# A new issue order for an attention, experts and mixing kernel whose instructions stay the same

## The chip, the cores and the metric

The kernel runs on one core of one Trainium2 chip. The metric is the device time of one execution in microseconds; where several executions are given, their median counts. The core has four compute engines that each work through their own stream of instructions in order: TensorE (PE, with its weight loads as PEld), VectorE (DVE), ScalarE (ACT) and GpSimd (POOL). SyncE (SP) issues transposing DMAs. They meet only at semaphores.

## The reference

Three layers follow one another, on 2 batches of 768 rows with 512 columns.

```python
# 1. attention of 8 heads (64 columns each) in which a query sees the keys of its own hash bucket
mask = q_bucket[:, :, :, None] == k_bucket[:, :, None, :]      # buckets: signs of q @ proj, k @ proj
scores = np.where(mask, scale * q @ k.T, -1e9); attn = softmax(scores); x = attn @ v
# 2. four causal attention experts (64 columns each), the best two of four weighted per row
logits = x @ w_gate;  y = sum over e of w_e * (softmax(causal(scale * (x@wq[e]) @ (x@wk[e]).T)) @ (x@wv[e])) @ wo[e]
# 3. channel mixing with the row before
xk = mu_k * y + (1 - mu_k) * y_prev; xr = mu_r * y + (1 - mu_r) * y_prev
out = sigmoid(xr @ w_r) * (np.maximum(xk @ w_k, 0) ** 2 @ w_v)
```

## The kernel before, in words

Numbers are split into a high and a low float16 part, and most products are three matmuls (high by high, high by low, low by high). Rows are worked on in 12 units of 128 (6 of each batch). A unit, with its number at the end of a tile's name, goes through these steps:

- `query_steps`: load q, split it (`naq`, `nbq`), turn it on PE (`tr_x2`, `tr_x1`) and copy it out by DVE (`x2`, `x1`). `key_steps` does the same for the keys of four heads (`nak`, `nbk`, `tr_y2`, `tr_y1`).
- `lsh_steps`: for each of 8 heads a score (`s`, 4 matmuls), the softmax (`softmax`: DVE reads the score out of PSUM into `P` with a running minimum, `mx`; ACT takes the exponential; ACT or POOL makes the high part of `PHL`, POOL the low part; an SP DMA transposes it into `PT`), then `pv` (`x`, 18 matmuls). `fin` divides and turns the result (`tr_x_`, `xT`).
- `moe_steps`: queries and keys of the experts (`proj_qk`: four groups of 12 matmuls, all in one tile `qk`, read out by ACT and DVE into `qT` and `kT`), values and gate (`vg`), scores (`se`), softmax, `pv` (`y`), `fin`, output (`o`).
- `mix_steps`: the shift (`m32k`, `m32r`, `mk`, `mr`), the hidden layer (`h`), the gate (`r`), the down product (`v`), the result `e`, and the store.
- `weight_steps`: weights are loaded and split once, by ACT, POOL and DVE (`split_w`, `split_d`).

PSUM has two pools. Scores (`s`, `se`) have two tiles of two banks each. Everything else that PE writes shares one tag with four tiles of one bank each:

```python
ps_s = Pool(... bufs=2, space=PSUM)   # [P, 2, 512] float32: two banks each
ps_d = Pool(... bufs=4, space=PSUM)   # [P, 512] float32: one bank each
```

In `turn`, a tile of up to 8 transposes is written in two halves of the same bank, and each half has its own copy:

```python
for j in range(2):
    for c in range(hn):
        nc.tensor.transpose(pt[j][:, c * P:(c + 1) * P], src[...], ident16)
    nc.vector.tensor_copy(dst[:, j * hn:(j + 1) * hn, :], pt[j]...)
```

In `fin` of `moe_steps` the sums of the softmax, their reciprocals (`rs`, profile name `y`) and the products with the gate (`rse`) use four columns of the bank of the tile `y`, into which `pv` accumulates.

Nothing of this is issued when it is written down. A `Program` records every instruction as an operation (consecutive matmuls of one step are one operation; there are 2673), and `arrange` reads a table, `ORDER`, which says in which order the operations are issued; `issue` then emits them at one line, so every row of the profile has line 188. An engine's stream is the table's operations of that engine, in the table's order. Dependences between engines become semaphore waits by that order. For a PSUM tile they go by bank: two accesses to the same bank by different engines are kept in the table's order, even where they touch different columns and neither needs the other's data. A wait stops all that stands behind it on its engine. All loads and stores are issued from ACT's stream (`LOADS = nc.scalar`), among its compute instructions.

Of the kernel before, what the change touches and what calls it, by code (L numbers as in the profile page):

```python
# [844 lines left out]
c-jru)3#tq5CG9cRc6&`+qP}r+qP}nwr$(CZQHhOyJvnOUiOOOPyhs?LKw&c`C%kX1OkA<&<65CJ}3wgp)HJp(J%(aLRy#vlVJ)JgXGW%3PBMl3gdtw1
VTXpAqsSZNYD|cLOX~I)1U;Dgmh2}N<#){4;{dOh4hdDQbJ?s4mH7nhg8r6hQfH50CiwGbb>N412RGYnV=kGhAa>bVnB3=30WZ<goT-q9l}F6hybzRHu
iv~&<uJ)4yXmapf>b{)KC}FKs<;Gi6IvZgM}~<VnaQM1M#6V+{2uZ1ae{mNR7Fn56ptzFdOdRU3`dTAr}sZE-(ic!3Y=xiy=4W!LHB`5<+uG1bHzZroq
857y3g*s02eG6K2NpkQUQnQb>;(uma4Xc`zUD<3`AWSuq<H#Rs?ql0kN?3XiZDR)dUK982I*D1Zg=F+RbkH~==mW+;T!p$3%1Wso03uqv*EYWM<Q;&OO
~^XWO}z{*es=F&W>i)FD4mclw%ms>z6u7JW=9k)OYTm`G4Cf34wxE1PS18j(m@D-NB()b$7<04uBKQIDqgDSXyDquydgb}GFMxw|Rg%(l~Tug7U39f-9
)DmjrPh3g|VJ-Z^sI(oF9IXRSZ}A<z$EFChjCR0sLRvx1F$Tq?m9&Z)V+;I^fABBX<N90~n_)m<h$tEzg8Hx%5>P8_jjdokBqXLbco^EEp|I2%jzBDmO  # L850
^GNDwZo&(kT-y(#PktAVRwv6$KU|<!p7W$cfmj04Sg^^HR5pe8B<bIJ`MwLHJyNtc#zgmGwy-S`6Tql6ttH5ViHP9d!Q%w!|QZ|4$&8Ek6-Z{?uCK4j@
FaV2Ks=Vuq$@MQ*atOU}x-t{c#_pp~IA%;?W=+jQe2(j>J(o8pq%`9FG%lBHpAS7@m^RWV{He=nM?Sv~+}y(pi{-Q*jzj$M1L!&cjaHMK|FRG~ji30fy
lLn2ED+HXf%FG#oF(6-Z6HDLSR2Ie3e%LJJ;?E%_GAz-y46GEhdk4GGL#Y{jj40p5Z0^bl^-Jj_KG=nhT7yKo)yQV8v#8*mR6VSY+%_R>iTrA@RLH&Z^
!N-v=yT%`N(2)58ZdH@CJ6fMEW@C5Et7J5LZsW26!r*MXjQ4U&&nJ6=5qgOB=3(;0uiqBvf7NLi<9A86rDoQ!&F7=bnyaKn;c6vr1;VgCGOH_s4z$1E0
Pv|w}rnivL6r()!4xYn)8o>?VJ-mQK<^#N>pRgKh(I@x}m+1;srB%2FSK?ai%H8-26sPrAjjB@(x<|j@H`J!*^pw8BMk+}gusnT(?@)q9@;2Owb*L_N=
O566U(r<xa3k)Z3RICs@o26@Z8(W3MWrd3*^U!9x!Hlca5w&eq~^XULw_L*Zo+>M76DV3lqQwgj9YLkzM*rJ+N3p)%tU@ci0Mpax<(D?EfLnFvNVY&^A
t{F+VVSkPvLM6?!$IGgBufLd+xvsI6O9_4^)nRQUr{MGdU90BZE!oftkg#+2S0Y%F}o+)+gru*pwQPU^8k??P(zYp@rOwe^Co+No}Y#wWW^SlVjsQQap
f$2eHFe<T0B$h)1v;4d%I=i5GEi9>a(5C?3P(2>h20V;}B7^LQ1PG{`IYHw|IS#63w^xfeMe%U#HGXNrtNISx+eVH|KL{!9<eV(w0TxgU3=PSk^zaCS4
C$MFgLLf`2VeWb56p5tOXjE_Gk0X{YTd4bJgzEOI!l%rr*ii(fT6I048=Y)6>FJVrT%j7oEIT0@7HGCPb;0lh0rA--A)|4{?_?dZb;&Kd*j$!zPS<Q(t
CdcB~JfGw6OA`ZQ;#$sN;&FUVzzI1Pp2n~oj>B^VZfMTnI*!P%Oh(hlWHOn}dVXUza3qe*Q8+4}#JA?Psc1HG5=@Gxu#!28=diKqO-Z<kX=--yLVF&Yn  # L860
Jgw5C*{R9)Lg);cnuSAG){)eF$ESjDe<ehjzvsSQ_LjhnkE(Az%9I+znSl*yt#>$O%+qs<T1s~R^H6DOma@adpRZV=d5OttzmZXPVPpVcpGo$Y9_C#ZG
M<KCZAbim)d3a0H@;oW*?{K<@OraHHW#LDPRhkLZ*T_$cOlkIl_DRD5v2Sc9p%uce#XVVeavL&cHv-FO!~E+O*u#jHYz_*Bs;He1hAWlibdn=6~iCH#c
p}7`o2YO)Ha;Gjlf1%USshU*y$xjRlLAY>3Iuaco?>)~>Vf%vnCi=Xn&>Hw{cYn}u`pd-K6O;7fd&ukcv9z<sH;X>W3I9|~jpQ&^jaZ}3fi%D4D7$F~V
=Li>c1*l{$0#?wUVV8YpsCcM3c5o|;|fcnuuGWMhCWO^HGAM#@sJCue|6x+`XF#XMN8bMe25f7pvW~dox2ARQTy<IJXX$VcC9GsKc4l{ksGk(s)%?LBn
j54FmC-d2S<ft~9olIZM4*P;P*q5w!qupeu&^md=Q|UENqmeY7X3!Sf#U!$Q%{Cj|ZnZOMr%h@*n_ae>iELw7XT9BS6Wdu7$p*H&>0!E>o~D<XP04I>o
55zZYh<nLw&`qH-fs`sLY%^mF_TO|4&eek*6g*Vd7q7GCz~lIl#6g-j%AB-8~tF*aTzYp6}bXe;y3(`-}77kz@PXJ|K!j7i@)$U-eXhRgZ7Z!Y!BNbcB
=Vl$C;xxwOub8WTR}7>E<_o<+S#gJ#J6flQtjc=ijESw$qRHlTBrdad9reo24YDvA^tZyH&QxA3N8S;(6wjJ#Ew5878*PWFOgocD$KjK(5-a_M1f^nQy
+^A2zf7Yd_m8Hmf~n&)Bn;MP#P2qB6~Vu?x&BGuz~|Mgn<ki`tm-#9p)4ZCJTs!^nAC%oemEwlY`Y3$`jd@v_W>+CsLlU2eijep|pkwMFbR``lLJ>Rf{
_+DrB?|KsAege_@H*_vF7OWQJbg{jR8O&qytmzu@qmc49aNqk8l31x@ul$<uaM3C?NgCj~Li7eZsy~dSzGSS?&ckEre$Rv`)l0>3NREZ|pY<4@xEHNw1
c1bT8B%|E3_w57w!sf86%xbg7ytJ=uF8kVc(hhpXrg!Nixx|p%wzFoE%#ua&*u3_Q?Wieaok=ONWxZKzHkgg3vqjTIGq{Ydt9H|}ww&E$D%+%zL%J)N&  # L870
1Rd~YId7FW{c^mY#!PgHko9VRFYcK$Xol)_R{E5)8>+Twhs5u?WVkaZ!6e}mP~HRF4yF`RIycUHG4zSN-bO4R=39dpWfV)`|?1X@#dz~vAblq>@wM;zH
MM{$!*CanOsA=NA}7?2~19TB#-5t<P|mV<%1lQe3D=GNdakM_sby(W5SxlQrGS^C#1MkvZbW7l#vQjQOZgq+uXLW<)pkEk;e9@gvv2FDW~MLoRPEgM4H
-y@=-oXC3z;#<%PVI^KwBhN=w_!wz44-&U}{M+DH599SLtnYGwH*RivuClGidyM{6}HD#fIb6qf38Ns7n;xht3DiVV`hIz+$AbnU18wY6<y+uDfcxYUq
(GE~n=1XDr=Xi4d4e@Q$0TOyhI(m;mkaBV1&O%xN=Je8V~)n#)#OlFtGy_F8Oz3pVX*siv(?QMJ5?zWGOW}=%Irm=LhEv1Qkk)M*?<#1Q!jr6lQT}%_p
jM1?=PWPD^`a{0TA9?4RN;7FLEu@yzmR8b9-n;cWQ)lUH?JQkngXVH|B)8jdVw<`W$HX=9%m~fn^12SP)BKfxvRqrs1Z^V+%tr^hLRV@#S*3H-YoHUgt
xVF%x=}ajW{s>h+y__FHIhRntag+r8dVRPDY`{#x!NwAwwL+Z({`1qdf0^52s&QFXhe;q(KNco(3l!azqqds^^^PTSd9+Ub-F-R7wR%yq>I(*5+$wU>b
h^Pl(YKXZPg!cy+2}(8qsdjT~_Nc)4`Q?Wn5XeRC`EAw_7{8a&C<tH}iClo-=dxyh)~MbeEQQ7tC36(Ofn^U2^^9`bb*6WO~UJ)7hod^twZPOHb)5{bj
hs*0s99Z}h+2CV#@j(UWGH#?^S*zzvh_TEWHFo!Zbfasy?6jF2v_t2<@lo6}~nB-CwM*!^)8-Co_NDKwEL)+E~4T{YLtel4gYWsp>Im0dn}KvQZe&F{{
bA(B8d>QFhUm-Mop(Q|rUTewqtR<CFV&7w_QOV`R3aHqAk+v>OZ&AyGhZf=;H=9al_QtK9<S(9o(SI=G0_U@uy)oXfPZ)j83*0pm*Tv3-*v*}IEu9-B4
ruJ$4cE7_Hav^S~zhmy2Vy?I=;c{v&&8_`yGgrk`{ht`|>i@a{c8}ld4{0@*SO5J##rd_5%cJ?UfELn{T3ACgRKxmS)_L#I1wO6s<w|G~P3OD0^!}h`@  # L880
IBpOJ)+08hbyk7w7MH?2ie}PqzmVdYIq;PNA!{WF}-I_=q-Jq5A~5g)~EVR$J^(6Tkq&yy{FyX5F6@t`7nN<eXVb_xqGYcG_%j*N6Bc3?1$Q6wy(?Tv-
$dNx9{f?`xp9BllY{5oPDp!d~!e0rtrh<2s_e_vax*}AJ_MH1KdD2!G6~JI>}D4lkHUdMZankAJs?mqwOd+){S@L++;V!W%oJ!H$_i=jLqanJN9GTQGd
)I_pkJWj<u=$RQJdaaf93^o!}<ANp6~(?q;}|ZkCJgWB8bUsC(?6=m<B>j&$*SeE(4s_?-T`4tB%bbUWOo^cj7A|3iOjQ9a>L`Wg0@KJlk~KEKQ@cPm^
0zs9X~>)an*@BZm*x6tMBzxA(zBPWiXcg6)SmQU#CxG-*!TkMv&xo)1@>b5!S=DVl<nSbu{`mk=Mz3i{}tA3W9ZRgmz_LKkYzxc1-_*{ODtaPi~1~<>1
@dsTZpW7Goul!h9;J*3q{<VMO3;7Tq>X*9tc8eP?XZ<-pM#jkmnIscsvfT2w{WX8x-|(e<6~E8Vl&Zd*FYhb(qJE>R=vTW<?vCH=w!0l}zrXA6`AWWwF
Y7D&YQDO!;Sczlezv^z@BDjT#25Cpd~ILc?{vG|Zdc3~)AN3o%$50a-_Mf;^1@G%sWMHbOG*FRm+~{Dgs<Z-_|h8A?REQH8Qt&pxC8ExJL*omgZ`%f=^
OdO?u<L)j=78ega6}Cxsz_8ERw}?$S;w99)bt{m#^!qYBjB{HMF@u?A!VlzMgOCTlvPmtX}dT{Sm)ZmPvj8!!MT=a@wzy@UES2@5^ZeUqQ=jMXjurw2G
>G=+C;pewDoR7}V0*N<kxStWA^y6NC$z_&Qos>uUHQVh}lq6hseV1QCLmK|O7t^|hh8K!Y$r*g%4&-UiLQ4}zenIv3f+50VDQU2EUQckms3vLHc_Fh~?
c3C_80K57sxh!vc0-F@;Pb`U3s8zc?}`FKGW-%Oip3+>@sYAa0@qz*C!X@aytL*Lm)a-Dov-_u8QF<dVn!S(iid=!^4$P}aqQU(cJf8Wpd^#lAsAJfHh
(Ohg7)kSx$HNK1M;<<z_kxS~5xxs$8ALWy~6fUt#;>P-vZir9iQoA@VjmsQl333KGf{X6FOY1JV3+}E<5@ZdA`JsM<PZy*QvIUo2uHcHh>e9I}ezYIwv  # L890
# [46 lines left out]
```

## Time and profile before

| | us |
|---|---|
| median of 3 runs | 549.61 |
| lowest, highest | 546.17, 550.96 |
| profiled execution, device time | 548.35 |
| its span, first to last instruction | 546.6 |

The mean granted TensorE clock over the span is 0.955 of full speed. In the profile's rows, "idle before" is the time in which an engine had nothing running ahead of an instruction, and the name behind the arrow is what ended that wait, read from semaphores. One execution is profiled; the runs were timed apart from it.

### The profile page before, as it was taken

The numbers are of one execution on the slowest core, as the hardware profiler recorded it, in microseconds if no ns is written. First come the engines' busy times: TensorE is split into PE (matmuls) and PEld (weight loads), VectorE is DVE, ScalarE is ACT, GpSimd is POOL, SyncE is SP. The second block draws the span as 40 slices with busy tenths as digits, with TensorE's granted clock in tenths as the row PEclk, the third lists the DMA queues.
The fourth block names the chain that finished last, engine by engine and source line by source line (L and its number), as shares of the span: only waits on it lengthen the run. The fifth ranks groups of instructions, "written<-read, shape, count | busy, mean of one in ns | idle before, by whom it ended". The sixth has DMA issues, their size and how long they took to land.

```text
span 546.6 us, 15654 instructions
## 1 busy us (share of the span) xinstructions
PE 449.4 (82%) x6288; PEld 340.4 (62%) x6288; DVE 378.3 (69%) x1094; ACT 353.2 (65%) x658; POOL 313.1 (57%) x286
## 2 busy tenths in 40 slices
...
GB/s 252 283 90 203 224 184 195 152 215 137 186 154 135 113 139 186 119 125 160 124 182 157 134 119 99 174 68 125 173 121 136 118 88 141 40 74 107 2 19 40
DMA packets 225240, 75.06 MB, mean 137 GB/s; under 512 B 216592, under 2 KB 220816, under 8 KB 225168
## 3 DMA queue, kind: packets, MB, share of 16 engines
...
## 4 chain that ended last, share of the span: by engine, by line
PE 48%; DVE 13%; DMA 8%; ACT 7%; issue 3%; POOL 1%; ACTq 0%; DVEq 0%; POOLq 0%; SPq 0%
PE v L188 10%; PE h L188 8%; DMA PT<-PHL 6%; PE s L188 5%; PE r L188 5%; PE x L188 5%; PE qk L188 3%; DVE P L188 3%; PE se L188 3%; ACT P L188 3%; PE y L188 2%; PE tr_x L188 2%; DMA PT_m<-PHL_m 2%; PE o L188 2%; PE vg L188 2%
## 5 line engine op out<-in xcount | busy, mean ns | idle before, releaser
L188 POOL TENSOR_TENSOR PHL<-P,PHL 128x768 f16<-128x768 f32 x96 | 159.5, 1667 | 65.2 <-ACT PHL L188 47.2
L188 ACT ACTIVATE P<-P,mx 128x768 f32<-128x768 f32 x96 | 89.1, 929 | 21.0 <-DVE mx L188 20.6
L188 DVE TENSOR_SCALAR_CACHE_REDUCE P<-s 128x768 f32<-128x768 f32 x96 | 91.2, 951 | 12.7 <-PE s L188 8.9
L188 PE MATMUL s<-y,x 128*128 128x384 f16 x384 | 80.2, 337 | 3.0 <-DVE P L188 2.8
L188 PE MATMUL x<-v,PT 128*128 128x64 f16 x1728 | 67.0, 197 | 12.6 <-DMA PT<-PHL 12.1
L188 PE MATMUL h<-mk,WK 128*128 128x128 f16 x1152 | 75.3, 221 | 0.0
L188 PEld LDWEIGHTS <-PT 128*128 128x128 f16 x1728 | 61.4, 101 | 20.2 <-DMA PT<-PHL 15.5
L188 PE MATMUL v<-WV,k 128*128 128x512 f16 x288 | 70.3, 391 | 0.9 <-ACT PHL L188 0.9
L188 PEld LDWEIGHTS <-WK 128*128 128x128 f16 x1152 | 68.9, 99 | 3.2
L188 POOL TENSOR_TENSOR PHL_m<-P_m,PHL_m 128x128 f16<-128x128 f32 (+5 forms) x48 | 49.6, 1037 | 35.2 <-ACT PHL_m L188 31.1
L188 ACT ACTIVATE PHL<-P 128x768 f16<-128x768 f32 x72 | 60.4, 842 | 10.6 <-DMA PT<-PHL 4.4
L188 PEld LDWEIGHTS <-x 128*128 128x128 f16 x576 | 41.1, 99 | 23.6 <-issue 6.6
L188 PE MATMUL qk<-xT,WQK 128*128 128x128 f16 x576 | 40.2, 227 | 16.9 <-DVE kT L188 6.7
L188 PEld LDWEIGHTS <-WQK 128*128 128x128 f16 x576 | 36.2, 102 | 19.6 <-issue 17.5
L188 PEld LDWEIGHTS <-k 128*128 128x128 f16 x288 | 27.9, 101 | 30.6 <-issue 3.7
L188 ACT ACTIVATE P_m<-P_m,bias_m 128x128 f32<-128x128 f32 (+5 forms) x48 | 31.7, 662 | 21.1 <-DVE P_m L188 20.9
L188 DVE TENSOR_SCALAR_CACHE_REDUCE P_m<-se 128x128 f32<-128x128 f32 (+5 forms) x48 | 28.7, 616 | 11.3 <-PE se L188 9.3
L188 PE MATMUL r<-WR,mr 128*128 128x512 f16 x144 | 35.6, 387 | 0.0
L188 PE MATMUL y<-vn,PT_m 128*128 128x64 f16 x504 | 23.1, 199 | 14.5 <-DVE rse L188 6.0
L188 PEld LDWEIGHTS <-PT_m 128*128 128x128 f16 x504 | 20.7, 102 | 19.2 <-issue 12.4
L188 POOL TENSOR_TENSOR mk<-m32k,mk 128x512 f16<-128x512 f32 x12 | 13.9, 1157 | 29.0 <-ACT mk L188 29.0
L188 DVE SCALAR_TENSOR_TENSOR h<-h,t 128x512 f32<-128x512 f32 x24 | 16.7, 696 | 17.0 <-ACT t L188 16.9
...
## 6 DMA issues: line engine op xcount, KB each, us to landing
...
PT<-PHL SPq DMA_TRANSPOSE x96, 4.7
```

Of the source, the lines that this page charges most:

```text
L188: getattr(getattr(self.nc, engine), method)(*[real(a) for a in args], **{k: real(a) for k, a in kw.items()})
```

## The change: another table for the same operations

Only `ORDER` is replaced. Both tables are permutations of the same 2673 operations (732 of PE, 938 of DVE, 577 of ACT of which 81 are DMAs, 282 of POOL, 144 DMAs of SP), and 44 places hold the same operation in both. In the making of the new table, accesses to one PSUM bank by different engines counted as ordered; in the making of the old one they did not. Which engine does what, the tiles, the number of buffers and the queue of the loads are unchanged.

```diff
 ORDER = """
-c-jru)3#tq5CG9cRc6&`+qP}r+qP}nwr$(CZQHhOyJvnOUiOOOPyhs?LKw&c`C%kX1OkA<&<65CJ}3wgp)HJp(J%(aLRy#vlVJ)JgXGW%3PBMl3gdtw1
...
+c-jq@gSKEv3;;VxC+WUp+qUiZ#<p$Swr$(CZQHhO&+bRmsj9Rlg9&5M6gPQHeq&5wGtrP4Y0{bWCbP+6@|t`m#HcA^ikjvo)L6r&gehqznaO5~nQEq)Q
...
```

The text is a compressed list of operation numbers. Decoded, it can be read by place. First the operations of the tile `tr_x2_7` (query turn of unit 7) in the old and the new table (place, engine, operation, output <- input), with what stands between them:

```
old  1239  PE   transpose x4   tr_x2_7 <- naq_7     (second half of the columns)
old  1240  DVE  tensor_copy    x2_7 <- tr_x2_7
old  1241  PE   transpose x4   tr_x2_7 <- naq_7     (the other half)
old  1242  DVE  tensor_copy    x2_7 <- tr_x2_7
new  1163  PE   transpose x4   tr_x2_7 <- naq_7
...
new  1168  PE   transpose x4   tr_x2_7 <- naq_7
new  1169  DVE  tensor_copy    x2_7 <- tr_x2_7
new  1170  PE   matmul x12     qk_4 <- WQK, xT_4
...
new  1172  PE   matmul x48     z_k1_0 <- y2_1_0, prhl
new  1173  DVE  tensor_copy    x2_7 <- tr_x2_7
```

Then those of the tile `qk_2` (queries and keys of the experts of unit 2), PE and ACT alone:

```
old   778  PE   matmul x12     qk_2 <- WQK, xT_2
...
old   791  ACT  activation     e_0 <- r_0           (sigmoid of unit 0)
old   792  PE   matmul x12     qk_2 <- WQK, xT_2
old   793  ACT  activation     kT_0 <- qk_2
old   794  PE   matmul x12     qk_2 <- WQK, xT_2
old   795  PE   matmul x12     qk_2 <- WQK, xT_2
old   796  ACT  activation     qT_2 <- qk_2
new   786  PE   matmul x12     qk_2 <- WQK, xT_2
new   787  ACT  activation     P_4_0 <- P_4_0, mx_4
new   789  PE   matmul x12     qk_2 <- WQK, xT_2
new   790  PE   matmul x12     qk_2 <- WQK, xT_2
new   793  PE   matmul x12     qk_2 <- WQK, xT_2
new   794  ACT  activation     kT_0 <- qk_2
new   795  ACT  activation     qT_2 <- qk_2
```

Places in which a PE operation follows, in the same bank, an ACT or DVE operation on other columns:

| tile | old table | new table |
|---|---|---|
| `tr_x` halves of the query turns | 14 | 11 |
| `qk` | 10 | 9 |
| `y` | 17 | 13 |

Between exponentials and sigmoids, which use different tables of ACT, the order of ACT changes 18 times in the old table and 16 times in the new one (the first load included).

## Rows read from the trace of the kernel before

**Rows 1.** The page: busy time, share of the span and instructions of each engine.
```profile
PE 449.4 (82%) x6288; PEld 340.4 (62%) x6288; DVE 378.3 (69%) x1094; ACT 353.2 (65%) x658; POOL 313.1 (57%) x286
```

**Rows 2.** Busy time by stretch: stretch, length, engines (instructions), clock, DMA share, GB/s.
```profile
50.00:75.00 25.00, 18.46 (x306) 13.76 (x303) 24.02 (x67) 23.15 (x42) 23.07 (x18) 1.00 1.07 205
...
0.00:154.00 154.00, 98.70 (x1334) 76.57 (x1335) 128.92 (x345) 101.42 (x192) 105.78 (x110) 0.92 0.88 193
154.00:546.60 392.60, 350.67 (x4957) 263.79 (x4955) 249.38 (x749) 251.76 (x466) 207.28 (x176) 0.97 0.67 116
...
268.70:294.00 25.30, 24.48 (x405) 19.23 (x402) 23.30 (x63) 22.91 (x43) 21.98 (x17) 1.00 1.05 174
...
436.60:461.60 25.00, 25.00 (x335) 17.49 (x334) 10.89 (x28) 16.50 (x29) 14.59 (x13) 0.94 0.65 114
```

**Rows 3.** Waits of PE: who waited for whom, us in total, times, longest.
```profile
PE tr_x L188 <- DVE x L188: 15.9, 9, 3.0
PE x L188 <- DMA PT<-PHL: 12.1, 13, 2.7
...
PE qk L188 <- DVE kT L188: 6.7, 4, 1.8
...
PE y L188 <- DVE rse L188: 6.0, 4, 3.2
PE qk L188 <- ACT kT L188: 5.6, 2, 3.9
...
PE qk L188 <- ACT qT L188: 2.9, 1, 2.9
...
PE s L188 <- DVE P L188: 2.8, 4, 1.2
```

**Rows 4.** Groups of PE instructions from 154 us on: busy, mean | idle before, releasers.
```profile
L188 PE MATMUL qk<-xT,WQK 128*128 128x128 f16 x447 | 30.3, 223 | 8.5 <-DVE kT L188 4.8 <-ACT qT L188 2.9 <-ACT e L188 0.4
L188 PE MATMUL y<-vn,PT_m 128*128 128x64 f16 x468 | 20.3, 197 | 11.4 <-DVE rse L188 5.2 <-DVE gs L188 2.9 <-DVE vg L188 1.3
...
L188 PE MATMUL tr_x<-consts,naq 128*128 128x128 f16 x56 | 5.7, 231 | 10.8 <-DVE x L188 10.0 <-DVE k L188 0.7
```

**Rows 5.** Timeline at two places: start, length, engine, operation [idle before].
```profile
150.73 1.28 ACT L188 ACT_TABLE_LOAD   x1
...
152.02 0.60 ACT L188 ACTIVATE e<-r 128x512 f32<-128x512 f32 x1
152.52 0.38 ACT L188 ACTIVATE kT<-qk 128x256 f16<-128x256 f32 x1
152.94 1.34 PE L188 MATMUL qk<-xT,WQK 128*128 128x128 f16 x12 [3.93 <-ACT kT L188]
...
237.17 0.42 DVE L188 COPY x<-tr_x 128x512 f16<-128x512 f16 x1
237.64 0.58 PE L188 MATMUL tr_x<-consts,naq 128*128 128x128 f16 x4 [2.70 <-DVE x L188]
```

**Rows 6.** Stretches of 3.4 us ahead of the half clock; then one at it, and their sum.
```profile
231.60:235.00 3.40, 2.27 (x70) 2.06 (x70) 2.26 (x4) 2.68 (x6) 3.17 (x3) 1.00 0.87 205
...
361.30:364.70 3.40, 0.66 (x14) 0.50 (x12) 2.41 (x10) 3.04 (x6) 3.03 (x3) 1.00 0.33 68
...
364.70:368.10 3.40, 3.40 (x12) 1.48 (x12) 2.36 (x10) 2.83 (x6) 2.84 (x3) 0.50 0.00 0
...
sum 23.80, PE 20.99 PEld 14.38 DVE 9.84 ACT 13.67 POOL 13.42; mean PE 3.50 PEld 2.40 DVE 1.64 ACT 2.28 POOL 2.24
```

**Rows 7.** The chain that ended last: the same 24 matmuls at two times (start, length).
```profile
152.94 2.62 PE qk L188 x24
...
337.76 1.35 PE qk L188 x24
```

**Rows 8.** Groups over the whole span: the pass out of a score; ACT's table loads.
```profile
L188 DVE TENSOR_SCALAR_CACHE_REDUCE P<-s 128x768 f32<-128x768 f32 x96 | 91.2, 951 | 12.7 <-PE s L188 8.9 <-POOL PHL L188 2.3 <-POOL PHL_m L188 0.9
...
L188 ACT ACT_TABLE_LOAD x18 | 23.1, 1283 | 4.8 <-issue 4.5
```

More of the change, by code (lines that the diff above doesn't have):

```diff
@@ L844 @@
 ORDER = """
[L845 to L890, printed above, removed]
@@ L891 @@
-j^AR4VOE}6XXr@1vlL-cg@{)`GW#M!JtqO5`+eYgCaq(piFSj-FJ7~1NX>1bR+#^H_y-a#e<1{ykFqw`m#ak;E5|2ln<V|XYRRs;a<8|ZjyiP7W&10vY
-+5f1Vw|AL8+i}P$gL8m-q_73_rzB^)vk}|He)8)BRgF+t2Y!{W4!KSngN&m4209?brC4!CJr0R}3lzRfB3l^`J)3AgCWS3>pPZg2qA9pjJ>js1q~`ng=
-a{mO-nab<ifL8?+7D1?_|X0P;~qZU
+c-jq@gSKEv3;;VxC+WUp+qUiZ#<p$Swr$(CZQHhO&+bRmsj9Rlg9&5M6gPQHeq&5wGtrP4Y0{bWCbP+6@|t`m#HcA^ikjvo)L6r&gehqznaO5~nQEq)Q
+l@~3XiA%6rl2WglABRxv<b`@GuC7@nM_Bs&~!50%ycuuh#6<fm<p!6DQB{pY$mF4CcDXHyy<SDnA~Q(nP4KB$R>x$X~LTbriH0#QkdHi!=yBI%p$Yc#5
@@ new lines @@
+B=NV-wwUHekY<swSLSVwRd7rkaUm;+i-no{4RinX;y(nQ5w<8m5bBWLlZlroM@95}2N*m#JlHo0Vp{xdQ`DDwEJ8GN~aA+=aR(Eu@2b<{or4iA@qS%Vd
+H%m>E`>ERYqNn1}EPnwr@rJ!F7YCMT>m_aPT#g9q>!+L+vs2j-Z$W}caEp1@ORW;U8WrlP52GD2R+4!zA9lLOY8b*8V$2UVdO95kuTGk5_nVLn!eq$Zi
+E0nec*6ocZB#%wa1O=VNX6o7(I2n+(&gj!G+>Ol#p4fUa|DG8;Z49vxOSQg4bX$XNu7z$OOFf7If&=49y1S}5=Ohk-?6`&<lgi5dg5f@@)d<C!J4Qw${
+Fh4B8Ww;cZ!$<f8pW%=>Z0gc-T!C*PD!zlJu+?lcKcEi$gkMkuR^loo`~qL0GAK5N-|!xqKr4ubM~p*{N6j(w4I0oN_zMAs!JXy+9>nW-1Gk$UrWwRQi
+;OMcq)CAFNU)*#2kXso(;C`9TS$rZDJJeRu`o8q!FJFdR%2KUhy6?k=x<J$4W^wrVG?3zXiUj*x7lM3VIoY7adEF{NR4PGwm17sCm3LEViQ_}O{qCuH2
@@ new lines @@
+X~wY({JGfN4diO?+I3UEqxAU^+rqXiaBL3rdRXu_bkb6nM^bhYgqpcVRE+4SnD+4uJ1)$wbG?CM}*fNALsmg`;@IjDTb~65`=i(+_T8c)X2wa1<QJ(Qw
+m@fgW(pTsId?Y8(jTU^kA32{6b^gr4xwOoAI`G7L5SVJ4iwK`<Dmzz~=P>tHs_fw7PZ(_v>C3VZODxox`8R7hY?;xOn+i{Oq)j~Or{-Zj%;I&`B)W;i@
+H^I<V;!tT_AHsT1nXXe3Xd}3aj`{sdpYL-AQ%!@PNnVAbAcnVKrejH{J+u`Ouel!m-6XwGL7>du$0@#8N@eH2F5$2UCh>!5Kd0`6S1uTq3Fbh7$g|HN!
+U{TzQxiKrgF&FWZ`D`-dIV^^6&0Tzn#W4?N!xDHFpW{9pY=)SvxDDT#_htfpG1>7cj-(IftNCdz;cNV6a^NUh203v#d^c6_4X%Jyuo8Zl?U>Leva2D9-
+H#2-WxRsP>_kdxliOOj0|WSFew#J07S_Wg8ckzpEWN@MHkG}HDeWIq6|Z7#tb=v&uh|IyOf{TL)v*Q|NNbN_I$ILAK`ER;rLjC#z-t%=YGNDO1REeMyu
@@ new lines @@
+i({1-1ghcGw9!pe>cbvY6V2gJ)O~D`7osN9`$%&1M_oF4zs>;Vni0fSGjPcA$3{5hB4Jm_;3_GDe0**ci)Uc1vJk0Wr*`IW(6RQUh#{Q)oXlL4ilMDZa
+-KsIZ9kLKKJ!<7gi3gZkJE55OUKU>$fENP}o99fTbACw8LdxR^@X7T6Mh;S$Pe2h$K*LA~gqJq*366|SN_)EbvkF8kQ#wms>oeP$Q%G<ss&VjFCSv0*%
+wvK{cbeQ96VjyRNtQA3;FX0Sc+5B8;g)SrkfF=e!$F_Ud%KjBBrY_r%e_#MAuFI-8#v9WDpo7!f!3x?X#_8Z25=@b{1(GLtm11J-%p?~-n4FPpRq#h{L
+9mCQ>4oBhX2t=aDq~yp`XY7hc;TRl;2oz8>h)z)`Dy^pI5CcxYD?6O#({f4-Z)^-Y4RPrVoP@P>3SQfo5DUKA#T=7j(K=dBZ*4qU#D#4%ib%034#k7Kw
+un6o=V1eFr1+G8E<$`b2Nxg#T!Ph-&*ryDATcF{WRQq1!xgv+MQt%#+$MxXkQ`D#8C%wtvq`9;tz=U|D!2yMAt6<^Nog1Dr2;k?6|{wHa@tKPC?(ajwQ
@@ new lines @@
+OyBn5x)rxP`XT4%$h1>=CMJtJxZMKOLZVwz+L%>)5)sp4~&6>6`s--`fv%6K$jIRNl6<f9zlT&)$Gkl-1sZqx8f6w7+bKtzfI$)3k(3*k#<nrlvHMj?&
+XUI!M>ZFfj5(x<r@h3T2=(be7IhTFOX==olTRrF?=;QY(9k&eL+PZ`;~CbeHbYN4id#DG%kQ?39<XQ9B!kSMW++#knX8wXm&if6Pj8_$saE`_vC_&{JB
+?&*(WlpbK=9KH6LKh}zpv_Oo5f9c)-$Cw=iYt>Ie`j^pwG>}WgLbvzI)55^}Hk2i2{yOD?3ht$vR;6b>FAJY&F&k^_q^~Rxgm`%dJ?Mr$^%&%!1=b%1z
+jcnoVJivajZ>gWe=dC=@_P2xVU_0E7uzl?t8fiz_cl4e<&?ovuf9N-Tqdpjsf6@ou$)9Po-DHR2FdU9KNq9GZp<VoyM&L+{!m&9r6Yu4<vY+>HS9^drN
+>on333)TGmkrX{M&g6KNj6JTPQ=}8GCs^(<q)UgHhPqg@D|y_%8oyCPut6$;%I!DJ)hu{{E<I#7n_))^D#coF*qi7w>@k+{>fkY41edd{Ed@y2F}PSI3
@@ new lines @@
+<7KF?Ot-WPkB*4tNxf!Lc~qPPS9*R681f@IN*J5{uLFBt#j96L36E#J@Zl=h{C^Vns!SB^B?GZStL_;1Aj<<Lr1l!OpYu?G4UHGwe(|%Pz3(HLQe_?UI
+_)b0&VokNF8-<=HkrEwjt*3L9P`NM_E$S@|5F=L<X)r{Q$G$+tKk7v+Lnh(kD(3$qh13+-*b!*}^9KjY_ojVIdc+*aFZelEZ<<uCoCVtkM9^8>!fm-sT
+zz?nD;i*pg4jU~7wm*Ub~h6_;~388{ifI=yj6s96nl+sHE$tbZUy(>n=sRWgzQWQuSi71gIJ4cqKc9BgkDI}$2lFX7t=GbhUgL85ReZjf-CFka8wlpoV
+ulO~0()iL*J8Kk)D$!)IU1{@hUQQt8sEc;fu9{F**)o();z~Rz%au8mq?R<Y+ODzX_zhp-vJ^uq(_4PWJ++r6lEjikqDywE!S%Q%KjbQuOv+PL>aIPsB
+2}PDRGuqvMZPEZ<$<J?oU+zd;i_DXYjJI^!@Fd+?2-E1oLg{9-eA|;b#|lOY`5EOcDLPQ_u5@{tIg!HN-nu3?>U<^;D&r%ZpeA5M%C$pT$C-gIyd1ORF
```

22 lines of the change are left out of this document (added).

## The prediction

> **What bounds the kernel now.** I read the page's busy shares first, then busy time by stretch, then who PE waits for, and last the timeline at single waits. PE is the busiest engine, 449.4 of 546.6 us, with DVE at 378.3, ACT at 353.2 and POOL at 313.1 [rows 1]. The 97 us in which PE has nothing are unevenly spread. Up to 154 us PE works 98.7 us and misses 55.3; DVE works 128.9 there, and between 50 and 75 us it works 24.0 of 25 [rows 2]. That first stage, with the weights' splitting, the first keys and the first softmaxes, hangs on DVE, and a PE wait in it often costs nothing. From 154 us on PE works 350.7 of 392.6, all others at most 251.8: there PE sets the end, and its 41.9 idle us are what an order can win.
>
> What ends these waits is the point. PE's longest sums are on DVE's copies out of `tr_x` (15.9 us), on DVE's and ACT's reads of `qk` (6.7, 5.6 and 2.9) and on DVE's small operations in `y` (`rse` 6.0) [rows 3]. None of these is a wait for data: the four transposes that wait for the copy of `tr_x` write the other half of its bank, the 12 matmuls of `qk` write other columns than ACT reads. The timeline shows the semaphore: the copy begins at 237.17, takes 0.42, and the transposes start at 237.64, 0.05 us after its end; ACT's read of `qk` ends at 152.90 and the matmuls start at 152.94 [rows 5]. So the order in which the old table put two accesses to one bank is enforced, and PE pays for it. From 154 us on these waits sum to 10.0 for `tr_x`, 7.7 for `qk` and 9.4 for `y` [rows 4]: 27 of the 41.9 us. Stretches without such a wait show what is left: 268.7 to 294 us has PE idle for 0.8 us, with DVE at 23.3 of 25.3; 436.6 to 461.6 for none [rows 2].
>
> **The clock.** From 153 us until the last store the granted clock falls to 0.50 (the 1.2 of the two levels, 1.2 and 2.4 GHz) in six stretches, 23.8 us in all, in which PE is busy 21.0 [rows 6]. Ahead of five of them PE had hardly worked; the row shown, 361.3 to 364.7, has 0.66 us of 3.4, and the others 0.16 to 0.56; ahead of the sixth it worked 2.27 [rows 6]. Each of the six stands at one of the longest same-bank waits (3.93, 2.70, 3.17, 2.74, 2.95 and 2.94 us; two of them in [rows 5]). The same 24 matmuls of `qk` take 2.62 us there and 1.35 later [rows 7], so 21.0 us of work at half clock cost some 10.5.
>
> **The change, part by part.** No instruction is added, taken away or moved to another engine; what moves is places, and with them the waits. I decoded both tables and, with each operation's duration in the profiled execution, summed the PE work that each table puts between two places.
>
> *Same-bank waits, removed.* In the old table six `tr_x` halves follow the copy of the first half with no PE work between the two; they waited 1.33 to 3.02 us, 2.2 on the mean (`tr_x2_7` of the decoded lines is one). In the new table 13 of 24 `tr_x` tiles have both halves ahead of the first copy, and the 11 others have 3.1, 0.0, 1.4, 1.3, 2.0, 1.2, 4.4, 3.8, 3.0, 1.2 and 4.6 us of PE work in between. Of a 2.2 us lag, 1.0 us stays exposed after the first stage (one place at 1.2). For `qk` the five old places with at most 0.2 us between waited 1.69 to 3.93, mean 2.4; the new ones after the first stage have 1.9, 1.2, 0.9, 2.2, 7.1, 0.7 and 1.5, which leaves 0.5 + 1.2 + 1.5 + 0.2 + 0 + 1.7 + 0.9 = 6.0. `y` is harder: its small DVE operations wait for exponentials and for each other, and PE's cover can't be read where none of the tile's matmuls stands ahead of them. There 9 places are left after the first stage; seven have no matmul ahead, as six had in the old table, of which three waited, 7.1 us in all. I take 4 (bounds 0 and 8). So 11 of 27 us stay: 16 won (bounds 10 and 25).
>
> *The half clock.* With no place over 1.7 us left by this count, most of the six stretches should go. I take 8 of 10.5 us (bounds 0 and 10.5), not all, since at 231.6 us PE had worked 2.27 of 3.4 and the clock fell all the same [rows 6]. The Trainium skill's page "TensorE: Matmul & The Clock Gate", Part 1, says that half rate is the default and that activity releases it. By that rule, with the waits gone, the whole 10.5 us would return and the sum would be 2.5 us lower.
>
> *The first stage.* Its PE stalls lie beside DVE work. Cut where PE's work reaches 8, 16, 24, 32, 40, 50, 60, 70, 85 and 100 us, and summing the busiest engine of each part, the old table needs 138 us there and took 154; the new needs 139. Same-bank waits of 13.1 us go for the most part, but another wait grows. Scores have two PSUM tiles, so a score waits until DVE's pass out of the one before the last (0.95 us [rows 8]) is over. At 12 places of the new table (2 of the old) PE's work between is shorter than that pass and what it waits for, by 16.1 us together (2.9 in the old), all ahead of 61 us of PE work. The two cancel: I take a gain of 2 (bounds +8 and -13). Waits for the transposing DMAs stay (19 places short by 27.9 us before, 21 by 26.7 now, nearly all in this stage).
>
> *Tighter stretches.* Cut the same way into parts of 25 us of PE work, the new table has four behind the first stage in which another engine has more to do than PE: DVE with 27.2, 26.4 and 25.4, and ACT with 27.3, its table loads of 1.28 us each [rows 8] not counted. The old table has one, DVE with 26.3. That costs some 5 us (bounds 2 and 10), given back as waits for softmaxes. Two ACT table loads fewer are 2.6 us of an engine that isn't the bound: nothing. The loads, in ACT's stream as before, mostly get longer leads; SP's 144 transposes move by at most 10 places among themselves; POOL's stream, 207 us busy from 154 us on [rows 2], has room. I cost these at nothing; without that room a late load would cost what stands behind it on ACT, some 4 us at the first use of a weight. Behind the last expert scores the new table has 74 us of PE work (60 in the old), all of it ready; the chain's last piece, the down product of unit 11 and its store, is the same.
>
> **Sum.** Gains 16 + 8 + 2, losses 5: 21 us. The profiled execution took 548.35, so 527.4; the median of the runs is 1.26 above the profiled one, so 528.6. I forecast 528. The bounds together, not all at once, give 512 to 540.
>
> **Rivals.**
> 1. *The waits come back.* PE gets ahead and stops at the next thing, `PT` or a score's buffer, since softmaxes are fed by DVE, ACT and POOL in turn. For it: PE waited 12.1 us for `PT` even now [rows 3]. Against: late stretches without same-bank waits run full. It would leave 3 us or less: 545 to 549.
> 2. *It is only another order.* If the waits in `tr_x`, `qk` and `y` were late for other reasons, ACT's read of `qk` behind a table load and a sigmoid, say [rows 5], the new table has its own such places: 540 to 558. That starts 0.05 us behind the semaphore speak against it for the old waits, not for new ones. The Trainium skill's page "PSUM — Partial Sum Buffer", section "PSUM bank collisions raise a hardware error", says that the chip does not arbitrate between two engines on a bank, so the program must wait: by that rule no new table can drop such a wait, only put work ahead of it.
> 3. *Slower: the score buffers decide.* PE's stream is in order; blocked at a score, it holds up the transposes and products behind it, and DVE and ACT run dry. The price is the 13.2 us by which the 12 places are shorter than the 2, in the first stage; the point from which it decides is where the later stage wins less than that. With no later gain: 563.
> 4. *All of it.* Nothing stays of the 27 us, the clock returns 10.5, little is given back: 508.
>
> **How the numbers follow.** Forecast 0.66, rival 1 0.12, rival 2 0.10, rival 3 0.07, rival 4 0.05. The range is 508 to 552: it leaves out rival 3 and the slow end of 2, and a little below. A measurement of this kernel can tell about 1% from no change. Faster by over 1% (below 544): 0.66 + 0.05, and some of 1 and 2, 0.76; within 1% 0.13; slower 0.11.
>
> **What the profile after would show.** Right: PE's waits on `x`, `kT`, `qT` and `rse` together below 16 us over the span (they are 37 in [rows 3]); fewer than four half-clock stretches after 150 us; PE idle after its first 100 us of work at 20 to 30 us in place of 42; that point reached at 147 to 160 us. The score waits on DVE's `P` should rise from 2.8, to no more than 15. Wrong: those waits gone and PE's idle time the same, now before `PT`, or the first stage over 165 us.

## The result and the profile after

| | before | after |
|---|---|---|
| median, us | 550.29 | 505.56 |
| lowest, highest, us | 546.17, 553.03 | 501.94, 508.05 |
| profiled execution, us | 548.35 | 506.95 |
| its span, us | 546.6 | 505.1 |
| mean granted clock | 0.955 | 0.968 |

Four runs of each; the ratio is 0.9188, 95% interval [0.9103, 0.9273]: 44.7 us less, where 21 were forecast. The time lies below the range, near the 508 of rival 4. Here and below a ratio leaves out runs that lie over 1.5% above the fastest of their kernel, and the medians don't.

The page after, the lines of busy time and of the granted clock in 40 slices of 12.6 us, beside [rows 1]:

```profile
PE 440.0 (87%) x6288; PEld 332.2 (66%) x6288; DVE 376.0 (74%) x1094; ACT 346.9 (69%) x656; POOL 311.3 (62%) x286
...
PEclk9997999697979999999999999999999999999999
```

The same instructions ran, two ACT table loads apart; PE's busy time is 9.4 us shorter because it ran at half clock less often, and its idle time fell from 97 to 65 us. Where, is read from busy time by stretch (columns as in [rows 2]), cut at 141.8 us since PE has then worked 98.7 us, as it had at 154 us before:

```profile
0.00:141.80 141.80, 98.73 (x1366) 74.11 (x1366) 126.08 (x339) 100.19 (x192) 105.82 (x110) 0.92 0.97 206
141.80:505.10 363.30, 341.30 (x4923) 258.06 (x4922) 249.91 (x756) 246.73 (x465) 205.47 (x177) 0.99 0.72 126
...
141.90:145.30 3.40, 0.00 (x0) 0.00 (x0) 3.11 (x18) 1.63 (x6) 2.79 (x3) 1.00 1.33 143
...
145.30:152.10 6.80, 5.42 (x50) 3.33 (x51) 0.50 (x3) 1.91 (x3) 2.39 (x3) 0.51 0.66 132
152.10:503.00 350.90, 335.86 (x4873) 254.74 (x4871) 246.20 (x738) 243.08 (x456) 200.19 (x171) 1.00 0.71 126
```

The span lost 41.5 us: 12.2 in the first stage (154 to 141.8) and 29.3 behind it (392.6 to 363.3). Of the 29.3, PE's idle time is 19.9 (41.9 to 22.0) and its busy time 9.4. The clock explains 7.8 of the 9.4: behind the first stage one stretch at half clock is left, 145.3 to 152.1, with PE busy 5.42 us, so 2.7 lost where 10.5 were lost before [rows 6]. The other 1.6 is mostly that the two tables don't have the same instructions behind the cut: by the cut of the table below, which counts equal work, the two gains are 13.8 and 27.7 us.

Who PE waits for, over the span, beside [rows 3]:

```profile
PE x L188 <- DMA PT<-PHL: 19.7, 15, 4.9
PE tr_x L188 <- DVE naq L188: 8.6, 2, 7.9
PE s L188 <- DVE P L188: 6.1, 6, 2.0
PE y L188 <- DMA PT_m<-PHL_m: 5.8, 5, 2.2
...
PE tr_x L188 <- DVE x L188: 1.9, 3, 1.1
```

And PE's groups behind 141.8 us, beside [rows 4]:

```profile
L188 PE MATMUL x<-v,PT 128*128 128x64 f16 x1242 | 47.2, 194 | 10.9 <-DMA PT<-PHL 10.6 <-ACT e L188 0.3
...
L188 PE MATMUL qk<-xT,WQK 128*128 128x128 f16 x433 | 28.3, 219 | 0.7 <-DVE qT L188 0.7
L188 PE MATMUL y<-vn,PT_m 128*128 128x64 f16 x468 | 18.8, 193 | 3.1 <-DMA PT_m<-PHL_m 3.1
```

Of the kernel before, from 154 us on, the first of these groups is

```profile
L188 PE MATMUL x<-v,PT 128*128 128x64 f16 x1242 | 46.7, 194 | 3.2 <-DMA PT<-PHL 3.1
```

The wait for the other half of `tr_x` was 15.9 us and is 1.9; in `qk` 0.7 us is left behind the first stage; `rse` is gone from the list. What is left in front of `x` and `y` are waits for data, the transposing DMAs, and those grew: from 3.1 to 10.6 us before `x`. The timeline of one query turn shows the new pattern (start, length, engine, operation):

```profile
206.19 0.61 PE L188 MATMUL tr_x<-consts,naq 128*128 128x128 f16 x8 [1.00 <-DVE y L188]
...
206.64 0.83 PE L188 MATMUL qk<-xT,WQK 128*128 128x128 f16 x12
...
207.31 1.34 PE L188 MATMUL z_k<-prhl,y 128*128 128x6 f16 x48
...
207.40 0.74 DVE L188 COPY x<-tr_x 128x512 f16<-128x512 f16 x2
```

All eight transposes run together, PE goes on to other banks, and DVE makes both copies 0.6 us later, when PE no longer needs that bank. In [rows 5] the copy stood between the two halves.

### The profile page after: what moved, and what is told of

The parts are those of the page before. It is cut to its first block, busy times and chain, and to the rows that moved or that the text cites. A ratio compares the mean times of both kernels' runs of the same rounds, so it can differ in the third digit from the quotient of the medians.

```text
span 505.1 us, 15642 instructions
## 1 busy us (share of the span) xinstructions
PE 440.0 (87%) x6288; PEld 332.2 (66%) x6288; DVE 376.0 (74%) x1094; ACT 346.9 (69%) x656; POOL 311.3 (62%) x286
## 4 chain that ended last, share of the span: by engine, by line
PE 40%; DMA 8%; DVE 7%; POOL 4%; ACT 4%; issue 3%; DVEq 0%; POOLq 0%; ACTq 0%
PE h L188 10%; PE v L188 9%; DMA PT<-PHL 6%; PE r L188 4%; PE x L188 4%; POOL PHL L188 3%; PE qk L188 3%; PE s L188 2%; DMA PT_m<-PHL_m 2%; PE se L188 2%; DVE P L188 2%; PE y L188 2%; PE o L188 1%; ACT P L188 1%; PE vg L188 1%
## 5 line engine op out<-in xcount | busy, mean ns | idle before, releaser
L188 PE MATMUL s<-y,x 128*128 128x384 f16 x384 | 83.2, 345 | 7.2 <-DVE P L188 6.1
L188 PE MATMUL h<-mk,WK 128*128 128x128 f16 x1152 | 71.5, 219 | 0.0
L188 PE MATMUL v<-WV,k 128*128 128x512 f16 x288 | 68.4, 379 | 0.0
L188 PEld LDWEIGHTS <-WK 128*128 128x128 f16 x1152 | 66.4, 98 | 2.6 <-DVE k L188 0.2
L188 PE MATMUL qk<-xT,WQK 128*128 128x128 f16 x576 | 37.3, 219 | 1.9 <-DVE xT L188 1.2
L188 PEld LDWEIGHTS <-WQK 128*128 128x128 f16 x576 | 34.0, 98 | 4.3 <-issue 2.1
L188 ACT ACTIVATE t<-h 128x512 f32<-128x512 f32 x24 | 14.2, 592 | 32.9 <-PE h L188 26.7
L188 DVE SCALAR_TENSOR_TENSOR h<-h,t 128x512 f32<-128x512 f32 x24 | 16.7, 695 | 24.8 <-ACT t L188 24.7
L188 PE MATMUL r<-WR,mr 128*128 128x512 f16 x144 | 34.2, 383 | 0.4 <-DVE e L188 0.4
L188 POOL TENSOR_TENSOR mr<-m32r,mr 128x512 f16<-128x512 f32 x12 | 14.4, 1200 | 22.3 <-ACT mr L188 22.3
```

The costliest lines, as they stand in the source:

```text
L188: getattr(getattr(self.nc, engine), method)(*[real(a) for a in args], **{k: real(a) for k, a in kw.items()})
```

## The experiments

All but the two of the last but one group compute the full result. The ratio is always to the kernel before, run on the same chip (its medians: 547.3 to 548.7 us). A name with underscores is a kernel; "moves" are edits of the table, shown by decoded places. One column needs a word: the first stage ends where PE has done its first 100 us of work, each operation valued by its duration before; by that cut the kernel before takes 155.6 us for it and the new table 141.8. The rest runs from there to the issue of the last store, some 2.6 us before the end of the span. Both are of the profiled execution, one for each kernel; two kernels have none that can be compared.

| kernel | median, us | ratio [95%] | first stage, us | the rest, us |
|---|---|---|---|---|
| before | | 1 | 155.6 | 388.4 |
| after | 505.56 | 0.919 [0.910, 0.927] | 141.8 | 360.7 |
| old_all | 517.27 | 0.944 [0.939, 0.949] | 146.7 | 365.6 |
| old_first | 542.36 | 0.990 [0.984, 0.996] | 149.0 | 389.5 |
| old_later | 522.41 | 0.954 [0.949, 0.959] | 157.6 | 360.8 |
| old_turns_qk | 525.14 | 0.957 [0.951, 0.963] | 147.7 | 376.3 |
| old_y_sbuf | 540.84 | 0.985 [0.978, 0.993] | | |
| old_tq_ysbuf | 519.00 | 0.948 [0.940, 0.957] | 146.9 | 366.0 |
| new_back | 519.87 | 0.948 [0.943, 0.953] | 145.7 | 369.4 |
| new_back_later | 516.51 | 0.942 [0.933, 0.952] | 143.1 | 366.7 |
| new_back_first | 513.00 | 0.928 [0.920, 0.936] | | |
| old_then_new | 518.35 | 0.944 [0.939, 0.950] | 156.9 | 358.3 |
| new_then_cover | 514.91 | 0.938 [0.931, 0.944] | 139.9 | 367.5 |
| cover_then_new | 517.13 | 0.945 [0.938, 0.952] | 151.3 | 366.4 |
| new_cover | 511.60 | 0.935 [0.927, 0.942] | 144.0 | 361.1 |
| old_light | 546.09 | 0.997 [0.992, 1.001] | 150.5 | 390.4 |
| new_light | 502.52 | 0.915 [0.908, 0.921] | 140.3 | 358.4 |
| cover_new_loads | 556.51 | 1.015 [1.006, 1.023] | 165.5 | 383.3 |
| new_old_loads | 555.03 | 1.014 [1.006, 1.023] | 177.1 | 372.6 |

**Only the same-bank places of the old table.** In old_all nothing of the old table moves but the operations at its same-bank places: 14 second halves of `tr_x`, 10 late groups of `qk`, and in 12 tiles the three small DVE operations in `y` behind its last product.

```diff
 PE   transpose x4   tr_x2_7 <- naq_7
+PE   transpose x4   tr_x2_7 <- naq_7
 DVE  tensor_copy    x2_7 <- tr_x2_7
-PE   transpose x4   tr_x2_7 <- naq_7
 DVE  tensor_copy    x2_7 <- tr_x2_7
```

old_first does this in the 9 tiles of the first stage alone, old_later in the 27 behind it, old_turns_qk in turns and `qk` everywhere but not in `y`.

> The old table with local moves alone: in 14 query turns the second half goes right behind the first, in 10 qk tiles the late matmul groups go ahead of the first read, in all 12 y tiles the three small DVE operations go behind the last matmul. No PE operation then follows another engine's access to other columns of its bank. Theory 1 (the waits of PE on a bank, 41 us, and the half clock behind them are what the change won): 505 to 518 us. Rival (the new order as a whole, its balance and its loads, won the time): 535 to 550 us.

> The same moves, only in the nine tiles of the first stage (tr_x2_0, tr_x1_1 to tr_x1_3, qk_0 to qk_2, y_0, y_1). The prediction's step, that DVE's work hides PE's waits there: 546 to 550 us. Theory 1, that they count in full, 13 us and some half clock: 533 to 540 us.

> The same moves, only in the 27 tiles behind the first stage. Theory 1 (27 to 29 us of waits and 10 us of half clock): 512 to 522 us. The prediction's own sum for that stage, 16 and 8 won and 5 given back: 528 to 534. Rival (order as a whole): 540 us or more.

> The old table with the local moves in the 14 query turns and 10 qk tiles, and the y tiles left as they were. If the waits count one by one, the y tiles' 9 to 11 us of waits stay and this lies 8 to 11 us above the kernel with all moves: 525 to 529 us. If moving the three small operations behind the last product only shifts the wait into the turn of y: 517 to 521 us.

old_all gives 31.4 of the 44 us, old_first 6.3 (between its two expectations), old_later 26.3: the two parts add up (32.6), and the part behind the first stage is larger than the 19 us (16 + 8 - 5) that the forecast gave it. In old_turns_qk the waits in `y` stay, and with them some 7 us (0.957 against 0.944). Its PE waits:

```profile
PE y L188 <- DVE rse L188: 6.6, 3, 3.2
...
PE y L188 <- DVE gs L188: 2.9, 1, 2.9
```

**The `y` waits without a move.** old_y_sbuf is the old table with the sums and their reciprocals in an SBUF tile of their own, so that DVE's small operations no longer touch the bank into which PE adds up (the weights `rse` lie in SBUF in every version); old_tq_ysbuf is the same with the moves in turns and `qk`.

```diff
-st["y"], st["rs"] = py[:, :E * D].rearrange("p (e d) -> p e d", d=D), py[:, E * D:E * D + E]
+st["y"] = py[:, :E * D].rearrange("p (e d) -> p e d", d=D)
+st["rs"] = sp.tile([P, E], F32, tag="rsy", name=f"rsy_{i}")
```

> The old table, not one place moved; the four columns for the sums of the softmax and their reciprocals lie in a tile of SBUF of their own in place of the bank of y, so DVE's small operations and PE's products of y no longer share a bank. If PE's waits there (some 11 us by the profile) are for the bank and count one by one: 537 to 541 us. If they are late data or come back at the next wait: 546 to 550 us.

> The old table with the moves in query turns and qk tiles, and the sums of y in SBUF in place of moving them. If the moves in y cost nothing: as with them, 515 to 519 us. If moving the small operations behind the last product cost what the new table with the same moves lost (6 us): 509 to 513 us.

Without any change of order the bank alone is worth 8.0 us (547.32 x 0.0146, with an interval of 4 to 12); with the other moves made, some 5 (0.957 against 0.948, with intervals that overlap). PE's waits for `rse` and `gs` before `y` are gone from the trace of old_y_sbuf. So the `y` waits were waits for the bank and not for the sums.

**The old pattern put back into the new table.** new_back splits 8 query turns by the copy again and puts readers back between the groups of 7 `qk` tiles; new_back_later has such places (14) behind the first stage only, new_back_first (10) in it only. Of `tr_x2_7`:

```diff
 PE   transpose x4   tr_x2_7 <- naq_7
-PE   transpose x4   tr_x2_7 <- naq_7
 DVE  tensor_copy    x2_7 <- tr_x2_7
+PE   transpose x4   tr_x2_7 <- naq_7
 DVE  tensor_copy    x2_7 <- tr_x2_7
```

> The new table with the old pattern put back in 15 tiles: in eight query turns the copy of the first half goes between the halves, in seven qk tiles one read goes ahead of the last groups, with no PE work between. Theory 1 (15 places at some 2.2 us, and half clock behind some of them): 535 to 548 us. Rival: below 515 us.

> The new table with the old pattern put back in 14 tiles behind the first stage, nine query turns and five qk tiles. At the 1.0 us a place that 15 tiles in both stages cost: 517 to 522 us. At the 2.2 us a place of the prediction: 533 to 538 us.

> The new table with the old pattern put back in ten tiles of the first stage alone: the query turns of units 0 to 3, qk_1 and qk_2. If DVE's work hides PE's waits there, as the prediction had it: 503 to 508 us. If they hold up DVE: some half of 10 us or more, 510 to 517 us.

PE's waits in new_back, against those of after above:

```profile
PE x L188 <- DMA PT<-PHL: 13.7, 15, 2.7
PE tr_x L188 <- DVE x L188: 9.7, 11, 3.1
...
PE qk L188 <- DVE qT L188: 2.6, 3, 0.9
PE qk L188 <- DVE kT L188: 2.5, 2, 1.4
...
PE qk L188 <- ACT kT L188: 1.9, 2, 1.5
```

The 15 places bring back 14 us of these waits (16.7 against 2.6), the time rises by about 14 (0.948 against 0.919 is 16, the medians differ by 14.3): 1.0 us for a place. new_back_later gives 10 to 13 us for 14 places (by the means, and by the ratios), 0.7 to 0.9 each. The wait for `PT` falls by 6.0 in return, so the waits are partly exchanged for each other, but not all. new_back_first lies 3 to 5 us above the new table for its 10 places (508.3 and 509.0 us in its ratio, and 0.928 against 0.919, with intervals that overlap): about half as much for a place as behind the first stage, and between its two expectations.

**Splices of the two tables.** old_then_new runs the old order up to 100 us of PE work and then the rest in the new order; new_then_cover the new and then old_all; cover_then_new old_all and then the new. new_cover is the new table with the same kind of moves at the places that it still has.

> The old table up to 100 us of PE work, then what is left in the new table's order. Where the stages' gains are separate (13.8 us and 27.7 us in the two profiles): 518 to 524 us. If the new table's later stage needs its own first stage to be free of waits: 528 us or more.

> The new table up to 100 us of PE work, then what is left in the old table's order with the local moves. If behind the first stage the same-bank waits are all that the new table won, this is as fast as the new table: 503 to 509 us. If the rest of its order matters there too: 512 us or more.

> The old table with all local moves up to 100 us of PE work, then what is left in the new table's order. If the new table's first stage is 5 us ahead for another reason than the same-bank waits: 509 to 513 us. If it's the local moves behind the first stage that cost the 12 us: 503 to 508 us.

> The new table with the local moves in all places that are left in it (11 turns, 8 qk tiles, the y tiles), save qk_0. Its profile has under 3 us of same-bank waits left, so the theory of waits says 503 to 508 us, no change that can be told; if the moves themselves cost something (small operations later, reads later) it is slower, 508 to 514 us.

The old first stage in front of the new rest loses 14 us against the new table (0.944 against 0.919), in the stage itself 15 (156.9 against 141.8). With the kernels above, the medians (us) can be set out by the order of the first stage and of the rest:

| first stage | rest old | rest old with moves | rest new |
|---|---|---|---|
| old | 547.3 to 548.7 | 522.4 | 518.4 |
| old with moves | 542.4 | 517.3 | 517.1 |
| new | not run | 514.9 | 505.6 |

The times don't add up: the new first stage in place of the moved one is worth 11.6 us before the new rest and 2.4 before the moved one. new_then_cover meets the expectation by which the rest of the new order matters behind the stage too; cover_then_new is slower than both of its expectations, and no faster than old_all. new_cover is slower than the new table by 6 us although it has fewer same-bank places (0.935 against 0.919, with intervals that just touch). So a move or a seam may have a price of its own; the times can't take it apart from the gain.

The stage itself can be read better, since up to the cut a splice issues the very operations, in the same order, of a table that ran before. The old first stage took 155.6, 156.9 and 157.6 us (before, old_then_new, old_later), the moved one 146.7, 149.0 and 151.3 (old_all, old_first, cover_then_new), the new one 139.9, 141.8 and 143.1 (new_then_cover, after, new_back_later). One order differs by up to 4.6 us from execution to execution (the other engines can be past the cut by then), and the three groups don't overlap. On the mean the same-bank moves take 7.7 us off the stage, and the rest of the new order another 7.4. Behind the cut the moved order (360.8, 365.6, 367.5) and the new one (358.3, 360.7, 366.4) can't be told apart in this way.

**Is the first stage hung on DVE?** old_light and new_light do two of the four DVE operations with which a weight of the last layer is split (`split_d`) on 8 columns only; the output is not the reference's.

```diff
-nc.vector.scalar_tensor_tensor(u, low, 29, u, op0=OP.logical_shift_right, op1=OP.bitwise_or)
-nc.vector.scalar_tensor_tensor(u, top, 0xC0000000, u, op0=OP.bitwise_and, op1=OP.bitwise_or)
+nc.vector.scalar_tensor_tensor(u[:, :8], low[:, :8], 29, u[:, :8], op0=OP.logical_shift_right, op1=OP.bitwise_or)
+nc.vector.scalar_tensor_tensor(u[:, :8], top[:, :8], 0xC0000000, u[:, :8], op0=OP.bitwise_and, op1=OP.bitwise_or)
```

> The kernel before with less work on DVE: of the operations that put a weight's 32 bits together, two of five do 8 columns in place of 512 (the low bits and the sign of most weights are left out, so the output isn't the reference's). That takes some 21 us of DVE's 129 us out of the first stage, and no wait of PE on a bank. If DVE's throughput binds that stage, as the prediction had it: 528 to 535 us. If what binds it are chains of waits from engine to engine: 540 to 549 us.

> The same cut in the new table (output again not the reference's). If the new table's first stage is bound by DVE, whose share there rose from 83 to 89%: 486 to 492 us. If not: 498 to 505 us.

Busy time by stretch (columns as in [rows 2], the third sum is DVE's) of old_light:

```profile
0.00:50.00 50.00, 25.56 (x333) 19.31 (x334) 36.76 (x90) 28.14 (x46) 37.34 (x44) 0.94 0.81 217
50.00:100.00 50.00, 35.41 (x501) 26.17 (x500) 36.40 (x131) 36.88 (x75) 36.47 (x36) 0.89 1.02 195
100.00:154.00 54.00, 39.36 (x562) 31.75 (x562) 37.72 (x132) 39.48 (x81) 32.65 (x32) 0.91 0.91 177
```

And of the kernel before, cut at the same times:

```profile
0.00:50.00 50.00, 24.71 (x315) 18.80 (x316) 40.21 (x83) 24.98 (x40) 35.19 (x42) 1.00 0.77 206
50.00:100.00 50.00, 35.26 (x522) 26.39 (x519) 44.51 (x136) 38.41 (x76) 38.07 (x37) 0.93 1.01 200
100.00:154.00 54.00, 38.73 (x504) 31.39 (x504) 44.21 (x129) 38.04 (x77) 32.52 (x32) 0.83 0.85 174
```

DVE has 18.0 us less to do in the first 154 us, and PE gets through 1.6 us more work in them. By the cut of the table the stage is 5 us shorter and the rest 2 us longer; the kernel is 2 us faster, or not at all (the interval holds 1.000). In the new table the same edit is worth some 3 us, with intervals that overlap, and its stage of 140.3 us lies among those of the new order above. An engine that can be relieved of 14% of its work for so little is not what the stage hangs on.

**The places of the loads.** cover_new_loads is old_all with its loads at the new table's places, new_old_loads the new table with the loads at the old one's.

> The old table with all local moves, and each of the 69 loads moved to where the new table has it, counted by the PE work issued ahead of it (as far as buffers allow). If the loads' places win what the new table's first stage is ahead by (some 5 us): 510 to 514 us. If not: 515 to 520 us, or more where a load now delays a compute instruction of ScalarE.

> The new table with each load moved to where the old table has it. If the loads' places matter: 509 to 515 us. If not: 503 to 508 us.

Each table with the other's loads is slower than before, and far above either expectation: 39 us above old_all, 50 above the new table. ACT's waits in new_old_loads, of which after has 0.6 us (`nak`), 2.1 (`wm_r`), 1.7 (`wm_k`), none for `v`, and 0.8 (`wm_v`):

```profile
ACT nak L188 <- DMA k<-in_k_dram: 15.0, 5, 5.1
...
ACT wm_r L188 <- DMA raw_r<-in_moe_w_r_dram: 10.3, 3, 3.7
ACT wm_k L188 <- DMA raw_k<-in_moe_w_k_dram: 9.3, 3, 4.6
ACT v L188 <- DMA v<-in_v_dram: 8.5, 4, 3.3
ACT wm_v L188 <- DMA raw_v<-in_moe_w_v_dram: 7.9, 3, 2.8
```

No version beats the new table with the full result: all that undoes a part of it is slower, and so is the further moving of new_cover.

## Why the prediction was wrong

The direction and the mechanism were right, and the size was half of what came. Taken by its steps:

**The waits belong to the order, and PE sets the end behind the first stage: right.** Moving 36 tiles' operations gave 31.4 us, taking `y`'s bank away 8.0 without a move, and putting 15 places back took 14. Rival 2 falls with that: the new table's own places hold it up for under 3 us.

**The failed step: "That first stage ... hangs on DVE, and a PE wait in it often costs nothing", and with it "The two cancel: I take a gain of 2".** It measured 12.2, beyond the bound of 8. PE's waits in the stage, before (to 155.6 us) and after (to 141.8):

```profile
PE tr_x L188 <- DVE x L188: 5.9, 4, 3.0
PE qk L188 <- ACT kT L188: 5.6, 2, 3.9
...
PE s L188 <- DVE P L188: 2.8, 4, 1.2
...
PE qk L188 <- DVE kT L188: 1.8, 1, 1.8
```

```profile
PE s L188 <- DVE P L188: 5.6, 5, 2.0
...
PE tr_x L188 <- DVE x L188: 1.9, 3, 1.1
```

The same-bank waits of `tr_x` and `qk` fell from 13.3 us to 1.9, as forecast. The 13.2 us that scores were to wait more for their buffers, and that were to cancel this, came to 2.8. Adding up by how much each place falls short treats the places as independent; in a stream in order a wait at one place gives the next its time. That last sentence is argued, not shown. By the prediction's own count the busiest engines need 138 us in the old table's stage and 139 in the new one's; the stage took 154 and 141.8, so it was the excess over this count that went.

The reading of [rows 2] was at fault too. The stretch from 50 to 75 us is full of DVE (24.0 of 25), but over the whole stage DVE was idle for 25.1 of 154 us. After the change it does nearly the same work (126.1 us) in 141.8, and old_light, with 18.0 us of it gone, has a stage 5 us shorter at most and a time that can't be told from that before. So DVE's throughput was a small part of the limit, and PE's waits could matter. They did, but not in full: taking 13 us of them away gave 6.3 in old_first, and putting ten places back cost 3 to 5 in new_back_first. "Often costs nothing" holds for about half of this wait time. The other half of the stage's gain, some 7 us by the comparison of the splices, is the rest of the new order; which part of it stays open.

**The mis-sized term: 11 of the 27 us stay.** Under 1 stayed: `qk` has 0.7 us there, and `tr_x` and `qk` together 2.6 over the whole span; `y` has none. The lag was taken as 2.2 and 2.4 us a place, the mean of those old places that had waited. Put back into the new table, a place costs 1.0 (new_back) and 0.7 to 0.9 (new_back_later). The lag of the old places is no price for a place in another order: in new_back the eleven waits on `x` sum to 9.7 us, 0.9 each, where the old ones were 2.2. So the 0 to 2 us of PE work that the new table has at its remaining places were mostly enough. About 26 us went in place of 16.

**The half clock: right.** 8 was taken, 7.8 came, and one stretch is left where fewer than four were forecast. Between 141.9 and 145.3 PE did nothing, waiting for `PT` (its longest wait, 4.9 us), and the clock stood at half from 145.3; from 152.1 to 503 it was whole (1.00). The Trainium skill's page "TensorE: Matmul & The Clock Gate", Part 1, by which activity releases the full rate, agrees with that: what kept the whole 10.5 from returning is one wait that the new table still has.

**Tighter stretches, 5 us: right.** Some 26 us of waits went behind the first stage and PE's idle time fell by 19.9: 6 came back, as rival 1 had it for all of them. They stand before `x`, where the wait for `PT` is 10.6 us behind the first stage (3.1 before the change), and before `y` (3.1 for `PT_m`).

**Loads at nothing: right for this change, and for a narrow reason.** That they moved together with their users may be why they cost nothing. Against the other table's computation the same places cost 39 and 50 us, ten times the 4 us that was named for a load too late.

**The signs.** Waits on `x`, `kT`, `qT` and `rse` together below 16: 2.6. PE idle behind the first 100 us of work at 20 to 30: 22.0. Score waits no more than 15: 6.1. All as said. The first 100 us of PE work by 147 to 160 us: 141.8, and that is the sign of the failed step. With the first stage's 2 replaced by 12.2, the 11 of idle time behind it (16 less 5) by 19.9 and 8 by 7.8, the sum is 40 of the 41.5 us.

**Rival 4 was near by luck.** Its 508 rests on all 27 us, a clock of 10.5 and little given back; with the first stage's 2 that is 39.5, and 510 from the median of 549.6. What came is 26, 7.8 and 12.2, with 6 given back. A term that it didn't have, the first stage, made up for those that it had too large.

**What stays open.** The local moves give 31.4 us, the new table 44. Of the 12 between, some 7 lie in the first stage (149.0 and 141.6 us, each the mean of three executions). Which of the new table's other exchanges save them, and how much of the remaining 5 is a price of the moves themselves (6 in new_cover), the splices couldn't tell. That it is due to counting bank accesses as ordered when the table was made isn't shown either: only that the table has few such waits, and what they cost.
